# A pre-LN attention and GeGLU block: placement of group 0's keys and queries, FFN chunks, Tanh GELU and the last slot changed

## The chip, the cores and the metric

The kernel runs on one core of one Trainium2 chip. The metric is the device time of one execution in microseconds (us), the median of several runs; lower is better. The engines of a core are named as in the profile: PE (TensorE, matmuls; PEld is its weight load), DVE (VectorE), ACT (ScalarE), POOL (GpSimd) and SP (SyncE, which here issues transfers). Each takes its instructions in the order in which the program lists them; between engines they wait on semaphores.

## The reference

One transformer block on x of 2048 rows and 640 columns in bf16, 32 heads of 20:

```python
def _A_ref(x, wqkv, wo):                       # H = 32, Dh = 20
    qkv = (x @ wqkv).reshape(B, S, 3, H, Dh).transpose(2, 0, 3, 1, 4)
    q, k, v = qkv[0], qkv[1], qkv[2]
    p = softmax(einsum("bhqd,bhkd->bhqk", q, k) * Dh ** -0.5)
    o = einsum("bhqk,bhkd->bhqd", p, v)
    return o.transpose(0, 2, 1, 3).reshape(B, S, D) @ wo

def _B_ref(x, w_gate, w_up, w_down):           # Df = 1728
    return (gelu_tanh(x @ w_gate) * (x @ w_up)) @ w_down

h = x + _A_ref(layernorm(x), wqkv, wo)
out = h + _B_ref(layernorm(h), w_gate, w_up, w_down)
```

## The kernel before

The program doesn't run loops on the chip. Python code lists every operation with its engine, an estimated length, a priority, its reads and writes and the PSUM banks that it takes and frees (`Sched.op`, which all operations pass through, so most lines of the profile are L403 or a helper's). `Sched.schedule` then plays a list scheduler through once: at each moment each engine takes the ready operation of the smallest priority (P_QK = 0 first, P_BG = 3 last), and the resulting order is written out, with semaphore waits, by `Sched.emit`. The order on the chip is therefore fixed; only the times are the chip's. When PE has too little to do the scheduler adds dummy matmuls (`warm`, `pad`) by the limits WARM_MIN and PAD_MIN. It keeps background matmuls off PE when the next QK is due, QK_LEAD before its exp.

The head: x comes in four loads of 512 rows, LayerNorm statistics are taken on DVE (for rows 512 to 1023 on ACT), applied on DVE into xn_p, transposed on PE and evicted to xnT by ACT or DVE (L650, L653). Then the keys and queries of head group 0 are projected (`proj_k`, `proj_q`, matmuls at L702, evictions at L737 and L740). Keys and queries lie in kt_all and qt_all as 32 rows for each of four heads: row 0 holds a constant, rows 1 to 20 the head's values. For group 0 they are copied there by SP transfers, four for each 512 keys and four for the queries. The query's row 0 is an upper bound of its scores, got from the largest key of each row (L730) and one matmul (L811), added by DVE at L815.

Attention: a group is four heads, a slot is 512 query x head-group units: all 2048 keys for one group and 512 queries, or two groups and 256, or four and 128. There are 32 slots of 64 tiles; a tile is 128 keys by 512 (queries x groups), one PSUM bank. QK tiles (L1001) go in turn to banks 0 to 2 and to banks 3 and 4 (in the slots of SIX to 0 to 2 and 3 to 5), and ACT takes one exp over all banks of a set, of 1536 or 1024 columns, into pts or pts2. Some quads (four tiles, one for each head) are done by DVE instead, with a polynomial (L925 and what follows); D_QUADS says how many in each slot. In the slots of DA_SLOTS the polynomial's last addition is done by a POOL transfer that accumulates, elsewhere by DVE. PV products gather in bank 6 (32 rows for each head, 21 columns of v of which the last is one); an epilogue copies bank 6 to osb, transposes it (L1098), divides (L1104, L1107) and writes o_nat.

FFN: when the last group of a query chunk is done, `post` transposes o_nat, multiplies by wo, adds x (L1146), takes LayerNorm, and lists the gate products (L1179, copied to SBUF at L1214), GELU, the up products (L1228) and the down products (`down`, L1259, L1263) as background work in the two or three banks that QK leaves. Chunks are SIZES = 512, five of 256, two of 128. GELU of a chunk is done on ACT in place, up to 2048 columns at a time, after all its gate products; MERGE puts chunk 1 with chunk 2. Gelu and exp need different tables, so each such visit is a table load, the gelus, and a table load. The last chunk (`tail`) runs after the last exp, with its gelu straight from PSUM (L1201, L1204). FFN weights lie over the attention's weights and xnT (regw); they are loaded after slot 7's projections.

Of the kernel before, what the change touches and what calls it, by code (L numbers as in the profile page):

```python
# [18 lines left out]
WARM_WIN, WARM_MIN = 3.4, 0.5  # L19
PAD_WIN, PAD_MIN = 3.4, 0.42  # L20
QK_LEAD = .65
PE_AGE = 1.5
SD_ALONE = .21
P_SD = 1
# [23 lines left out]
class Sched:  # L48
# [48 lines left out]
    def schedule(self):  # L97
# [23 lines left out]
        while done < total:  # L121
            assert events, "no operation can start"
# [3 lines left out]
            for e in ENGINES:  # L126
# [122 lines left out]
                for o in ([o, join] if join is not None else [o]):  # L249
                    o.start = t0 if o is chosen else free[e]  # L250
                    if e == "act":
                        due = t + o.dur + (0.905 if o.dur > 1.2 else 1.332) - QK_LEAD if o.mode == "exp" else None
# [27 lines left out]
    def emit(self, es, block_of):  # L280
# [3 lines left out]
        prog = {e: [] for e in ENGINES}  # L284
        for o in self.order:
# [8 lines left out]
            for d in o.deps:  # L294
                q = ops[d]
                if q.eng == "pe" and o.eng == "pe":
                    continue
                k, c = q.pos
                if k not in need or need[k].pos[1] < c:
                    need[k] = q  # L300
# [50 lines left out]
SIZES = (512, 256, 256, 256, 256, 256, 128, 128)  # L351
BASE = (0, 0, 2, 0, 2, 0, 2, 3)
SIX = tuple(range(8, 12))
CHUNKS = tuple((sum(SIZES[:i]), n) for i, n in enumerate(SIZES))
NF = (DFF + 127) // 128
# [10 lines left out]
D_LAG = 8  # L366
MERGE = (1,)
DA_ISSUE, DA_LAT = 0.95, 6.4
DA_SLOTS = (1, 2, 3, 5) + tuple(range(9, 32))
PR, PR2 = 12, 6  # L370
D_QUADS = (1,) + (2,) * 11 + (3, 2) * 3 + (2, 2, 3) * 3 + (2,) * 5
D_FIRST, D_PART = 2, 0.55
D_LEAD = ((0,) * 8, (0, 10, 20) + (36,) * 21)
D_WIDE = 18
RSQRT_MAGIC = float(0x5F3759DF)

P_EV = 1.8
P_QK, P_PV, P_PRO, P_EPI, P_LN, P_BG = 0, 1, 1.5, 2, 2.5, 3
P_LND, P_LNP = 1.9, 2.5


def bass_sequential_preLN__mha_block__glu_gated_geglu__prompt_kernel(
# [12 lines left out]
    with ExitStack() as es:  # L395
# [13 lines left out]
        def c_act(n):  # L409
            return 0.052 + n * 0.000833  # L410
# [8 lines left out]
        off0 = sb("off0", [128, 1], FP32)  # L419
        stats = sb("stats", [128, 4, 2, 6], FP32)  # L420
# [3 lines left out]
        asum = sb("asum", [128, 2, 4], FP32)  # L424
# [49 lines left out]
        xn_p = carve(4 * D).rearrange("p (i d) -> p i d", i=4)  # L474
# [50 lines left out]
        def cst(fn, key, n=128):  # L525
            op(POOL, fn, 0.1 + n * 0.001, P_BG, writes=[key, "pool"])
# [5 lines left out]
        op("act", I("activation", f32(qt_all[:, 1, :, :]), zer[:, 0:2].bitcast(FP32).to_broadcast([128, 2048]), ACT.Copy), 1.8, P_QK,  # L532
           reads=["zer"], writes=["qf1"])
        op("act", I("activation", f32(qt_all[:, 2, :, :]), zer[:, 0:2].bitcast(FP32).to_broadcast([128, 2048]), ACT.Copy), 1.8, P_QK,
           reads=["zer"], writes=["qf2"])
        op("act", I("activation", v_all[:, :, :, DH], zer[:, 0:1].unsqueeze(2).to_broadcast([128, NT, H]), ACT.Copy, bias=1.0), 0.5, P_QK,
           reads=["zer"], writes=["vones"])
        op("dve", I("memset", f32(kt_all[:, 1:4, :]), ones2), 4.2, P_QK, writes=["kf0"])
        cst(I("memset", kt_all[:, 0, :].bitcast(FP32), ones2), "ktm0", 1024)
# [815 lines left out]
```

## Time and profile before

| | us |
|---|---|
| median of 3 runs | 910.08 |
| lowest, highest | 909.8, 910.76 |
| span of the profiled execution | 906.4 |
| ACT busy | 877.0 (97%) |
| PE busy | 832.6 (92%) |
| DVE busy | 740.7 (82%) |
| POOL busy | 123.5 (14%) |

The span runs from the first to the last instruction of the profiled execution; no time of its own with what lies around it is shown, so the runs' median stands beside it, 3.7 above. Busy time is the union of an engine's instructions; a row of the timeline gives start, length, engine, line, operation, what is written and read, and in brackets how long the engine sat idle before it and which instruction ended that. A group's row gives count, busy time and mean length of one in ns. The granted clock of TensorE was 1.0 throughout.

### The profile page before, as it was taken

The numbers are of one execution on the slowest core, as the hardware profiler recorded it, in microseconds if no ns is written. First come the engines' busy times: TensorE is split into PE (matmuls) and PEld (weight loads), VectorE is DVE, ScalarE is ACT, GpSimd is POOL, SyncE is SP. The second block draws the span as 40 slices with busy tenths as digits, with TensorE's granted clock in tenths as the row PEclk, the third lists the DMA queues.
The fourth block names the chain that finished last, engine by engine and source line by source line (L and its number), as shares of the span: only waits on it lengthen the run. The fifth ranks groups of instructions, "written<-read, shape, count | busy, mean of one in ns | idle before, by whom it ended". The sixth has DMA issues, their size and how long they took to land.

```text
span 906.4 us, 25256 instructions
## 1 busy us (share of the span) xinstructions
PE 832.6 (92%) x11167; PEld 376.8 (42%) x11167; DVE 740.7 (82%) x1405; ACT 877.0 (97%) x793; POOL 123.5 (14%) x238
## 2 busy tenths in 40 slices
PE   3999999999898988999999999999999998998998
PEld 2432322222233332334344445444444444656666
DVE  8858898989899997898898877787977996778643
ACT  7899999999999999999999999999999999999992
POOL 5001110000013111111222000030101000101000
PEclk9999999999999999999999999999999999999999
DMA  7213341442634322243263221441432332242110
GB/s 261 84 32 80 69 97 31 106 105 62 198 136 77 56 52 48 48 69 73 49 115 63 48 44 29 84 85 41 93 63 43 75 69 39 58 85 56 33 41 16
DMA packets 52357, 65.97 MB, mean 73 GB/s; under 512 B 20876, under 2 KB 38376, under 8 KB 52248
## 3 DMA queue, kind: packets, MB, share of 16 engines
q0 software_dynamic: 12816, 31.46, 19.4%
q1 hardware_dynamic: 39432, 32.89, 13.2%
q8 instruction: 88, 1.44, 0.7%
q14 instruction: 21, 0.17, 0.1%
HBM read 20.12 MB, written 8.09 MB: 31 GB/s over the span
## 4 chain that ended last, share of the span: by engine, by line
ACT 82%; PE 13%; DVE 4%; POOL 1%; issue 0%
ACT pts L403 52%; ACT rege L403 28%; PE ps L702 4%; PE ps L1001 3%; PE ps L1179 2%; PE ps L403 2%; ACT L403 1%; PE ps L1259 1%; DVE dwx L403 1%; DVE qt_all L925 0%; PE ps L644 0%; DVE rege L1228 0%; ACT qt_all L403 0%; POOL nw L403 0%; DVE rege L925 0%
## 5 line engine op out<-in xcount | busy, mean ns | idle before, releaser
L403 ACT ACTIVATE pts<-ps 128x1536 bf16<-128x1536 f32 (+1 forms) x474 | 565.3, 1373 | 3.9 <-PE ps L403 2.9
L1001 PE MATMUL ps<-qt_all,kt_all 32*128 32x256 bf16 (+2 forms) x4096 | 308.9, 272 | 39.1 <-ACT pts L403 18.1
L403 ACT ACTIVATE rege<-ps 128x1536 bf16<-128x1536 f32 (+1 forms) x233 | 292.7, 1379 | 0.5 <-PE ps L403 0.4
L1001 PEld LDWEIGHTS ps<-qt_all,kt_all 32*128 32x128 bf16 x4096 | 102.4, 92 | 252.8 <-ACT pts L403 128.6
L1179 PE MATMUL ps<-rege,regw 128*128 128x256 bf16 (+2 forms) x1120 | 159.2, 274 | 10.2 <-ACT rege L403 2.7
L403 PE MATMUL ps<-pts,v_all 128*21 128x256 bf16 (+2 forms) x2370 | 124.8, 274 | 0.0
L1179 PEld LDWEIGHTS ps<-rege,regw 128*128 128x128 bf16 x1120 | 86.1, 98 | 62.5 <-issue 27.6
L925 DVE TENSOR_SCALAR rege<-ps 128x512 int16<-128x512 f32 x120 | 81.9, 686 | 22.2 <-PE ps L1001 21.1
L925 DVE TENSOR_SCALAR qt_all<-ps 128x512 int16<-128x512 f32 x104 | 71.2, 686 | 27.1 <-PE ps L1001 26.4
L403 PE MATMUL ps<-rege,v_all 128*21 128x256 bf16 (+2 forms) x1366 | 91.1, 278 | 0.1
L702 PE MATMUL ps<-regw 128*128 128x512 bf16 (+1 forms) x360 | 87.5, 353 | 1.9 <-ACT regw L650 1.5
L1259 PE MATMUL ps<-regw,rege 128*128 128x320 bf16 x448 | 83.8, 302 | 2.5 <-DVE qt_all L925 0.7
L403 DVE TENSOR_TENSOR qt_all<-qt_all 128x1024 int16<-128x1024 f16 (+3 forms) x77 | 68.7, 893 | 1.1
L403 PEld LDWEIGHTS ps<-pts,v_all 128*21 128x21 bf16 x2370 | 54.8, 91 | 32.7 <-issue 27.8
L403 DVE TENSOR_SCALAR qt_all<-qt_all 128x1024 int16<-128x1024 int16 (+3 forms) x106 | 57.9, 549 | 1.6 <-DMA qt_all<-dwx 0.4
L403 DVE TENSOR_TENSOR rege<-rege 128x1024 f16<-128x1024 f16 (+1 forms) x74 | 50.4, 681 | 0.7
L1259 PEld LDWEIGHTS ps<-regw,rege 128*128 128x128 bf16 x448 | 36.4, 98 | 35.0 <-issue 16.6
L403 PE MATMUL ps<-kt_all,zer 128*32 128x512 bf16 x568 | 48.3, 385 | 0.0
L403 DVE TENSOR_SCALAR rege<-rege 128x1024 int16<-128x1024 int16 (+2 forms) x113 | 47.8, 437 | 0.4
L702 PEld LDWEIGHTS ps<-regw 128*128 128x128 bf16 x360 | 28.9, 99 | 44.1 <-issue 24.4
L1214 DVE CAST rege<-ps 128x512 bf16<-128x512 f32 (+1 forms) x53 | 35.9, 678 | 13.3 <-PE ps L1179 13.1
L1228 DVE TENSOR_TENSOR rege<-rege,ps 128x512 bf16<-128x512 bf16 (+1 forms) x53 | 35.7, 676 | 12.2 <-PE ps L1179 12.1
(114 smaller groups left out, 766.2 us busy)
## 6 DMA issues: line engine op xcount, KB each, us to landing
qt_all<-qt_all POOLq DMA_DIRECT2D x9, 512.0 KB, 5.0
qt_all<-dwx POOLq DMA_DIRECT2D x9, 512.0 KB, 4.6
rege<-rege POOLq DMA_DIRECT2D x16, 256.0 KB, 3.5
rege<-dwx POOLq DMA_DIRECT2D x7, 512.0 KB, 4.8
rege<-in_A_x_dram SPq DMA_DIRECT2D x5, 640.0 KB, 5.7
dvx<-qt_all POOLq DMA_DIRECT2D x6, 512.0 KB, 4.8
q_rows<-regw SPq DMA_DIRECT2D x20, 128.0 KB, 2.8
out_dram<-rege SPq DMA_DIRECT2D x16, 160.0 KB, 3.2
```

The source lines that it names most:

```text
L403: return lambda eng: getattr(eng, method)(*args, **kwargs)
L702: yield op("pe", lambda eng, l=l, r=r, k=k: eng.matmul(bank(bk, n), l, r, start=(k == 0), stop=(k == len(steps) - 1)), c_mm(n) + cold, pri ...
L925: d_ops.append(op("dve", lambda eng: eng.tensor_scalar(v[:, 512 * h:512 * h + 512], bank(b), EXP_MUL, -32000.0, ALU.mult, ALU.max), c_dve( ...
L1001: return lambda eng: eng.matmul(out()[:, kk * nq:(kk + 1) * nq], kt_all[32 * j:32 * j + 32, g, kt * 128:(kt + 1) * 128], qt_all[32 * j:32 ...
L1179: op("pe", lambda eng, a=a, f=f, fi=fi: eng.matmul(bank(bk)[:, fi * nq:(fi + 1) * nq], w[:, a, F0[f]:F0[f] + 128], hnT[:, a, 128 * tb:128 ...
L1214: cp.append(op("dve", lambda eng, bg=bg, fv=fv, w=w: eng.tensor_copy(fv, bank(bg, w)), c_dve(w), p, reads=[kg], writes=hkeys(k), rel=[bg], ...
L1228: hdone.append(op("dve", lambda eng, bu=bu, fv=fv, w=w: eng.tensor_tensor(fv, fv, bank(bu, w), ALU.mult), c_dve(w), p, reads=[ku] + hkeys( ...
L1259: op("pe", lambda eng, f=f, o=o, hf=hf, bk=bk: eng.matmul(bank(bk, 320), ha_f[:, o:o + 128], wd[:, f, hf * 320:(hf + 1) * 320], start=(f = ...
```

## The change

- *Group 0.* The queries and the last 512 keys (PERM_C = 3: keys from 1536 on) are put into the 32-row layout by a matmul with a permutation matrix `perm`; for the queries it accumulates in the bank of the bound. Keys 0 to 1535 are still copied by transfers. wk, wq and wv are loaded apart, wk first, and K's last 512 keys of group 0 are projected tile by tile.
- *Head.* LayerNorm statistics: of each four tiles the last 1, 1, 3 and 1 on ACT (LN1_ACT). Seven tiles are applied on POOL (LN1_POOL), nine evictions of xnT are on DVE (T_DVE), xn_p has eight buffers, small LayerNorm operations go to POOL. The fills of qt_all that ACT did go to POOL behind the applies, with the fills of kt_all's groups 4 to 7.
- *Chunks and slots.* SIZES = seven of 256 and two of 128. Slots 0 to 5 are groups 0 to 5 with 512 queries, slots 6 and 7 groups 6 and 7 with queries 0 to 255 and 256 to 511, so chunk 0 can be posted after slot 6. SIX is empty. The last slot is split: groups 4 to 6, then group 7 alone. D_QUADS sums to 70 (before 69); DA_SLOTS has 19 slots (before 27).
- *Weights.* w_gate is laid over wv, wk and k_un and asked for in slot 4 in pieces; w_up and w_down follow in pieces after slot 7.
- *GELU.* MERGE = (0, 2). For chunks 4, 6 and 7 (TANH) it is 0.5 g (1 + tanh(...)) with the polynomial on DVE and one Tanh for each bank of 512 columns on ACT, in rounds of the buffers that qt_all lends.
- *Order.* The last chunk's work has priority P_END = 0.5; its eviction of transposes is on DVE, wo's first four contraction steps run before the last group is there, and the down matmuls don't wait for the last product. The root of the LayerNorm takes eps as a bias. Constants of the scheduler change (WARM_MIN, PAD_MIN, QK_LEAD, PE_AGE, D_LAG and priorities), and POOL operations now wait for the one before.

```diff
-WARM_WIN, WARM_MIN = 3.4, 0.5
-PAD_WIN, PAD_MIN = 3.4, 0.42
-QK_LEAD = .65
-PE_AGE = 1.5
+WARM_WIN, WARM_MIN = 3.4, 0.53
+PAD_WIN, PAD_MIN = 3.4, 0.46
+QK_LEAD = 0.55
+PE_AGE = 0.5
...
-                        due = t + o.dur + (0.905 if o.dur > 1.2 else 1.332) - QK_LEAD if o.mode == "exp" else None
+                        due = t + o.dur + (0.905 if o.dur > 1.2 else 1.332) - QK_LEAD if o.mode == "exp" and o.tag[0] == "P" else None
...
-SIZES = (512, 256, 256, 256, 256, 256, 128, 128)
-SIX = tuple(range(8, 12))
+SIZES = (256,) * 7 + (128, 128)
+SIX = ()
+PERM_C = 3
+FIRST = 6
+QR = ((0, 512),) + CHUNKS
-D_LAG = 8
-MERGE = (1,)
+D_LAG = 4
+MERGE = (0, 2)
+TANH = (4, 6, 7)
+W_EARLY = 4
+P_END = 0.5
+P_LATE = 3
+P_TANH = -1
-DA_SLOTS = (1, 2, 3, 5) + tuple(range(9, 32))
-D_QUADS = (1,) + (2,) * 11 + (3, 2) * 3 + (2, 2, 3) * 3 + (2,) * 5
+DA_SLOTS = (0, 1, 10, 11, 12, 14, 15, 16, 17, 18, 19, 20, 22, 23, 24, 26, 27, 28, 31)
+D_QUADS = (0, 2, 2, 2, 2, 2, 2, 1, 2, 2, 2, 2, 3, 2, 3, 2, 3, 2, 3, 2, 3, 2, 3, 2, 3, 1, 4, 2, 3, 2, 2, 2, 0)
+T_DVE = (0, 1, 3, 5, 9, 11, 12, 13, 14)
+LN1_ACT = (1, 1, 3, 1)
+LN1_POOL = (0, 1, 3, 5, 6, 13, 14)
-P_EV = 1.8
+P_EV = 1.5
-P_LND, P_LNP = 1.9, 2.5
+P_LND, P_LNP = 1.7, 1.9
...
-        op("act", I("activation", f32(qt_all[:, 1, :, :]), zer[:, 0:2].bitcast(FP32).to_broadcast([128, 2048]), ACT.Copy), 1.8, P_QK,
-           reads=["zer"], writes=["qf1"])
...
+        for g in range(4, NG):
+            cst(I("memset", kt_all[:, g, :].bitcast(FP32), ones2), "kf%d" % g, 800, e_ops)
+        for k in range(1, 4):
+            for g in range(0, NG, 2):
+                cst(I("memset", f32(qt_all[:, k, g:g + 2, :]), 0.0), "qf%d%d" % (k, g), 512, e_ops)
...
+                e_ops.append(ln_apply(POOL if t in LN1_POOL else "dve", x_sb[:, t, :], xn_p[:, t % 8, :], ("xnp", t % 8), t, [f"x{t // 4}"], P_PRO,
                                       first=True))
...
+            if t == 0 and c == 3:
+                for tt in range(4):
+                    for a in range(NA):
+                        w_readers.append(op("pe", lambda eng, tt=tt, a=a: eng.matmul(
+                            bank(bk)[:, 128 * tt:128 * tt + 128], wsrc[:, a, 0:128], xnT[:, a, c * 512 + 128 * tt:c * 512 + 128 * tt + 128],
...
+                if t == 0 and c >= PERM_C:
+                    w_readers.append(op("pe", lambda eng, bp=bp, src=src: eng.matmul(bank(bp), perm[:], src, start=True, stop=True), c_mm(512), prio,
+                                        mode="full", util=0.213, reads=[("ku", 0, c), "perm"], writes=[kp], acq=[bp]))
+                    dst = kt_all[:, 0, 512 * c:512 * c + 512]
...
+            w_readers.append(op("pe", lambda eng: eng.matmul(bank(bk), perm[:], q_un[:, 0, :], start=True, stop=False),
...
-            q_first.append(op("dve", lambda eng: eng.scalar_tensor_tensor(
-                out=dst, in0=bank(bk), scalar=off0[:, 0:1], in1=dst, op0=ALU.add, op1=ALU.add), c_dve(512) + 0.05, prio,
+            q_first.append(op("dve", lambda eng: eng.tensor_scalar(dst, bank(bk), off0[:, 0:1], None, ALU.add), c_dve(512), prio,
...
-        for c, (q0, nq) in enumerate(CHUNKS):
+        for c, (q0, nq) in enumerate(QR):
             n = 512 // nq
-            slots += [(c, tuple(range(g, g + n))) for g in range(0, NG, n)]
+            slots += [(c, tuple(range(g, g + n))) for g in (range(FIRST) if c == 0 else range(FIRST if q0 < 512 else 0, NG, n))]
+        slots[-1:] = [(slots[-1][0], slots[-1][1][:-1]), (slots[-1][0], slots[-1][1][-1:])]
...
+            elif c in TANH:
+                for k0 in range(0, nb, nt_):
+                    for k in range(k0, min(k0 + nt_, nb)):
+                        bg, kg = mms(k, wg, "wg", tuple(x for key in hkeys(k) for x in sc.rd.get(key, ())))
+                        op("dve", lambda eng, bg=bg, fv=fv, w=w: eng.tensor_scalar(fv, bank(bg, w), 0.5, None, ALU.mult), c_dve(w), p, reads=[kg],
+                           writes=hkeys(k), rel=[bg], after=first)
+                        d(I("tensor_tensor", z, f2, f2, ALU.mult), 0.53, hkeys(k), [tk], aft)
+                        d(I("tensor_scalar", z, z, 8 * 0.044715 * GELU_C, 2 * GELU_C, ALU.mult, ALU.add), 0.265, [tk], [tk])
+                        d(I("tensor_tensor", z, z, f2, ALU.mult), 0.53, hkeys(k) + [tk], [tk])
+                        tanhs.append(op("act", I("activation", z, z, ACT.Tanh), c_act(w) + 0.04, P_TANH, mode="exp", reads=[tk], writes=[tk]))
+                    for k in range(k0, min(k0 + nt_, nb)):
+                        bu, ku = mms(k, wu, "wu", (sc.lw[tk],))
+                        op("dve", lambda eng, bu=bu, z=z, w=w: eng.scalar_tensor_tensor(
+                            out=z, in0=z.bitcast(F16), scalar=1.0, in1=wide(bank(bu, w)), op0=ALU.add, op1=ALU.mult), c_dve(w), p,
+                           reads=[ku, tk], writes=[tk], rel=[bu])
+                        hdone.append(op("dve", I("tensor_tensor", wide(fv), wide(fv), z, ALU.mult), 0.066 + 0.53 * w / 1024, p,
+                                        reads=[tk] + hkeys(k), writes=hkeys(k)))
...
+                if g == W_EARLY:
+                    pieces(wg, B_w_gate.rearrange("(a p) f -> p a f", p=128), "wg", tuple(w_readers))
```

344 lines of the change are left out of this document (209 added, 135 removed).

## The prediction

> **What bounds the kernel now.** I read the page first, then the busy time by stage, then ACT's instructions by shape, then the chain of waits at both ends.
>
> ```profile
> span 906.4 us, 25256 instructions
> ...
> PE 832.6 (92%) x11167; PEld 376.8 (42%) x11167; DVE 740.7 (82%) x1405; ACT 877.0 (97%) x793; POOL 123.5 (14%) x238
> ...
> L403 ACT ACTIVATE pts<-ps 128x1536 bf16<-128x1536 f32 (+1 forms) x474 | 565.3, 1373 | 3.9 <-PE ps L403 2.9
> ...
> L403 ACT ACTIVATE rege<-ps 128x1536 bf16<-128x1536 f32 (+1 forms) x233 | 292.7, 1379 | 0.5 <-PE ps L403 0.4
> ```
>
> ACT is busy for 97% of the span, and its 474 + 233 = 707 exps are nearly all of it. The stages, cut at the first exp and at the end of the last:
>
> ```profile
> core 0: us, PE busy (x) PEld busy (x) DVE busy (x) ACT busy (x) POOL busy (x), PEclk, DMA share, GB/s
> 0.00:32.86 32.86, 18.43 (x138) 10.71 (x138) 27.93 (x82) 27.49 (x48) 12.83 (x36) 1.00 0.58 195
> 32.86:876.01 843.15, 788.99 (x10700) 345.91 (x10699) 701.25 (x1295) 838.60 (x731) 110.63 (x202) 1.00 0.33 70
> 876.01:906.40 30.39, 25.15 (x331) 20.15 (x330) 11.55 (x30) 10.91 (x14) 0.00 (x0) 1.00 0.04 13
> ```
>
> In the middle ACT idles 843.15 - 838.60 = 4.55 us. So three things set the time: the head (32.86), ACT's own list in the middle, and the tail (30.39).
>
> **The middle, term by term.** From the chain of waits (start, length, what) and ACT's timeline and shapes:
>
> ```profile
> 742.85 4.52 ACT pts L403 x4
> ...
> 874.65 1.34 ACT rege L403
> ```
> ```profile
> L403 ACT ACT_TABLE_LOAD x16 | 20.5, 1283 | 1.1 <-PEq L1340 0.8
> L403 ACT ACTIVATE rege<-rege 128x2048 bf16<-128x2048 bf16 x8 | 15.0, 1904 | 0.1
> ...
> L403 ACT ACTIVATE rege<-rege 128x1536 bf16<-128x1536 bf16 x5 | 7.3, 1467 | 0.0
> ...
> L1201 ACT ACTIVATE dvx<-ps 128x512 bf16<-128x512 f32 x3 | 1.8, 597 | 4.7 <-PE ps L1179 4.7
> ```
> ```profile
> 539.54 1.28 ACT L403 ACT_TABLE_LOAD   x1
> 540.83 6.46 ACT L403 ACTIVATE rege<-rege 128x2048 bf16<-128x2048 bf16 x4
> 547.31 1.28 ACT L403 ACT_TABLE_LOAD   x1
> ```
>
> Two exps of three banks and two of two banks take 4.52, so a pair takes 2.26; a three-bank exp alone advances the chain by 1.34, a two-bank one by 0.92: each further bank costs 0.427, an instruction by itself 0.063. Laying out the tiles by SIZES, PAT and D_QUADS gives 358 exps of three banks and 349 of two before (707, as on the page), worth 800.1 us. With the new lists it gives 354 and 353: the list sums to 70 DVE quads against 69 (although the title says 69), so four tiles of 0.427 leave ACT: **-1.7**. SIX goes, but its three-bank pairs were worth only the 0.063 of the instructions they spared, which these counts hold.
>
> Gelu: four instructions over 2 x 2048 + 2 x 1536 = 7168 columns took 6.46, so 256 query rows (3584 columns) cost 3.23. Before the last exp the old kernel gelus 1792 rows = 7 such, 22.6; the new one 1280 rows = 5 such: **-6.5**. The 512 rows of chunks 4 and 6 become 14 Tanh of one bank; by the pitch above 0.063 + 0.427 = 0.49 each, and chunk 7 gives 3.5 more (it was a gelu after the last exp): **+8.6**. The nearest single row, L1201's 512 columns, is 0.597 with its own drain, so the upper end is +10.5.
>
> Table loads: 16 in all, one ahead of the head, one for the first exp, four after the last exp, so ten in the middle: five gelu visits of two. MERGE (0,2) and TANH (4,6,7) leave three visits (chunks 0+1, 2+3, 5): four loads of 1.28 fewer, **-5.1**, and the drain beside each, (838.6 - 800.1 - 22.6 - 12.8) / 10 = 0.31: **-1.2**. The lower end is the loads alone. The row prices a switch at 1.28 + 0.31. The Trainium skill (ScalarE: Activation LUTs, "What ACT_TABLE_LOAD costs") gives about 2.66 for every switch, drain included; by that the four would be worth 10.6, not 6.3; the measured lines decide.
>
> Sum of ACT's list: 838.6 - 1.7 - 6.5 + 8.6 - 5.1 - 1.2 = 832.7. Idle time:
>
> ```profile
> 42.23 4.63 ACT L403 ACTIVATE pts<-ps 128x1536 bf16<-128x1536 f32 x4 [2.48 <-PE ps L403]
> ```
>
> This one stall is over half of the 4.55. The seventh exp reuses the first slots of pts and waits for the first PV, which stands behind V projections that hold bank 6 until DVE empties it. Slot 0 now has no DVE quad, so DVE empties it sooner; I take the stall away and put 2 us for Tanhs that stand at ACT's head before DVE's polynomial is done: 4 in all, bounds 2 and 10. **Middle: 836.7.**
>
> What hides the rest is DVE's slack. Each Tanh bank adds four SBUF operations on 512 columns, and 24 quads instead of 9 lie outside DA_SLOTS and add on DVE again:
>
> ```profile
> 560.00:876.00 316.00, 300.28 (x5119) 162.53 (x5111) 247.59 (x401) 315.48 (x276) 38.17 (x82) 1.00 0.31 62
> ```
> ```profile
> L403 DVE TENSOR_TENSOR rege<-rege 128x1024 int16<-128x1024 int16 x14 | 9.5, 681 | 0.1
> ```
>
> At half of 0.68 the Tanh banks cost 18 x 4 x 0.34 = 24.5, and nine of the fifteen quads fall here, two adds each: 12.3. That is 284 of 316, below ACT's 315; at the full 0.68 it would be 309, and the cover is gone.
>
> **The head.** DVE, ACT and PE lines, in time order:
>
> ```profile
> 2.19 3.69 ACT L403 ACTIVATE qt_all<-zer 128x2048 f32<-128x2048 f32 x2
> ...
> 22.40 5.47 ACT L650 ACTIVATE regw<-ps 128x640 bf16<-128x640 bf16 x9
> ```
> ```profile
> 22.19 1.57 DVE L403 TENSOR_SCALAR rege<-rege,mu,rs 128x640 bf16<-128x640 bf16 x4 [0.94 <-PE ps L644]
> ...
> 27.35 0.49 DVE L653 COPY regw<-ps 128x640 bf16<-128x640 bf16 x1
> ...
> 29.82 0.68 DVE L730 TENSOR_REDUCE kd<-ps 128x1 f32<-128x512 f32 x1
> ...
> 31.53 0.75 DVE L815 SCALAR_TENSOR_TENSOR qt_all<-ps,off,qt_all 128x512 bf16<-128x512 f32 x1 [0.30 <-PE ps L811]
> ```
> ```profile
> 27.15 3.98 PE L702 MATMUL ps<-regw 128*128 128x512 bf16 x22
> ```
> ```profile
> L403 ACT ACTIVATE rege<-rege 128x640 bf16<-128x640 bf16 x8 | 6.2, 770 | 0.1
> ```
>
> ACT and DVE both work nearly without a gap until the last xnT is evicted at 27.84; then come K's matmuls, the peak, the bound, the first QK: 5.0 more. ACT loses the two fills (3.69) and six evictions of 5.47/9 = 0.61 (3.65) and gains two tiles of statistics, four passes of 0.77 and their read-outs (3.5): net -3.8. DVE loses seven applies of 1.57/4 = 0.39, two tiles of statistics and most small operations, and gains six evictions of 0.49: net about -2. The 0.94 wait for a free xn_p buffer goes with eight of them. I put the last eviction 2.3 earlier, the engine with the smaller relief deciding. Behind it K's matmuls for keys 512 to 1535 no longer stand, and the last 512 keys go tile by tile: of the 22 matmuls (0.18 each) some ten leave, 1.7. **First exp at 28.9, -4.0.** POOL's seven applies are not in this trace; the nearest rows are the 0.39 on DVE and POOL's 0.95 for a fill of 1024, so 0.6 by length, and I take no delay. Lower end nothing gained, if POOL is late with them; upper end -6.4, ACT's whole 3.8 plus 0.94 and 1.7. The permutation matmul itself replaces four q copies and four K copies on SP and turns the 0.75 into a plain add; with the keys it places needed only at tile 48 and later, it shortens the path by next to nothing. The fills moved behind the applies on POOL are needed only when group 1 starts, 29 us after the first exp (slot 0's exps); they take 4 x 0.95 + 12 x 0.55 = 10.4:
>
> ```profile
> L403 POOL MEMSET kt_all<- 128x1024 f32 x5 | 4.8, 951 | 0.3
> ...
> L403 POOL MEMSET qt_all<- 128x512 f32 x7 | 3.8, 550 | 0.4
> ```
>
> **The tail.** Chain of waits after the last exp:
>
> ```profile
> 878.82 1.71 ACT rege L403
> ...
> 881.36 1.43 PE ps L702 x10
> ...
> 885.71 0.93 DVE rege L1228 x2
> ...
> 886.72 3.28 PE ps L1259 x23
> ...
> 891.07 8.01 PE ps L1179 x140
> ...
> 899.58 3.99 PE ps L1259 x28
> ```
>
> The gelu, L1228 and the x23 are the second-last chunk's FFN, in the way of the last chunk's residual, LayerNorm and eviction: 1.71 + 0.93 + 3.28 = 5.9 of the chain. I give back 1.5 for steps of the last chunk that ran beneath them (transposes, root, apply): 4.4. With its FFN at P_LATE against P_END = 0.5, with no table visit, and with the chain of FFN chunks starting earlier, that goes. The chunks run one behind another, and the first gate matmuls stand here:
>
> ```profile
> 280.00:305.00 25.00, 6.65 (x22) 1.49 (x22) 1.00 0.38 68
> ```
>
> The 25 us before hold none. With weights requested at slot 4 they can begin at slot 8, whose begin the exps of slots 0 to 7 put at 28.9 + 208 = 237, so some 45 us are won against a lag that the last chunk still feels. Splitting the last slot leaves one group for the end: of the ten wo matmuls two remain (-1.1), and copy, transposes, scale and eviction shrink by about 1.8. The down matmuls no longer wait for the last product (-0.1 to -0.5). **Tail: 30.4 - 4.4 - 2.9 - 0.1 = 23.0**, bounds 22 and 27 (only the split).
>
> **Sum.** 28.9 + 836.7 + 23.0 = 888.6 against the span of 906.4, 17.8 less. The three runs have a median of 910.08, 3.7 above the span, which I keep: **892.3**. Changes under 0.2% (1.8 us) can't be told from none.
>
> **The rivals.**
>
> *Half of it* (20%): POOL's applies are late, so the head stays at 32.9, and FFN backlog still spills behind the last exp, 27: 32.9 + 836.7 + 27 + 3.7 = 900.3. For it: DVE falls out of DA_SLOTS more often, so background products slow down. By the Trainium skill (SBUF — State Buffer, "Who interferes with whom") a DVE operation in a two-port mode blocks GpSimd for its whole length, which speaks against applies on POOL beside DVE's; no row here shows it.
>
> *QK comes too late* (6%), slower. QK_LEAD falls from 0.65 to 0.55, so background matmuls may run 0.1 us further into the gap before a QK:
>
> ```profile
> 746.51 0.40 PE L1001 MATMUL ps<-qt_all,kt_all 32*128 32x256 bf16 x6
> ```
> ```profile
> 746.98 2.65 ACT L403 ACTIVATE rege<-ps 128x1536 bf16<-128x1536 f32 x2
> ```
> ```profile
> PEld ps L1001 <- ACT pts L403: 128.6, 351, 1.6
> ```
>
> Here the QK ended 0.07 before its exp began, so 0.1 later would hold ACT. At 0.06 for each of the 354 three-bank exps that is 21 us: 888.6 + 21 + 3.7 = 913. It turns the sign from 17.8/354 = 0.05 each. Against it: 351 times PE already stood waiting for ACT, 0.37 on average, so most gaps aren't filled up to the limit.
>
> *Tanh isn't in exp's table* (2%): then the change doesn't save loads but adds up to 18 pairs of 1.6, 58 us: some 950. The trace has no Tanh. The Trainium skill (ScalarE: Activation LUTs, "Table sets: the hidden batching unit") lists tanh in exp's set, which is why this stays small.
>
> **How the numbers follow.** Forecast 70% (own range 886 to 898 from the bounds of head, idle and tail), half of it 20%, slower ways 8%, some other way to no change 2%. Range 885 to 904. Faster 0.9, within 0.2% 0.02, slower 0.08.
>
> **What would show it.** First exp near 29; 10 table loads instead of 16 and none between a Tanh and an exp; 354 + 353 exps at 2.26 a pair; ACT idle between first and last exp under 6; last exp to end near 23, with no gate or up matmul of the second-last chunk in it. It is wrong if ACT's idle sum passes 10 (QK or Tanh late), or if the first exp isn't earlier.

## The result, and the profile after

The changed kernel takes 898.77 us (897.65 to 899.58) against 909.98 before on the same chip, a ratio of 0.9876 (95% interval 0.9862 to 0.989). It is faster, by 11.2 us where 17.8 were predicted, and 6.5 us above the predicted 892.3. From the page, the span and the engines:

```profile
span 897.2 us, 26288 instructions
...
PE 837.0 (93%) x11645; PEld 401.2 (45%) x11679; DVE 773.3 (86%) x1452; ACT 864.7 (96%) x799; POOL 123.4 (14%) x244
```

The busy time by stage, cut as before at the first exp and at the end of the last (columns: stretch, length, busy PE, PEld, DVE, ACT, POOL, granted clock, DMA share, GB/s):

```profile
0.00:32.38 32.38, 19.58 (x152) 12.35 (x156) 25.72 (x64) 24.95 (x50) 23.09 (x60) 1.00 0.58 190
32.38:869.50 837.12, 792.63 (x11172) 368.29 (x11201) 735.19 (x1358) 834.30 (x741) 100.33 (x185) 1.00 0.30 62
869.50:897.20 27.70, 24.83 (x325) 20.51 (x323) 12.35 (x31) 5.45 (x10) 0.00 (x0) 1.00 0.08 26
```

| stage | before | predicted | after |
|---|---|---|---|
| head, to the first exp | 32.86 | 28.9 | 32.38 |
| middle, first exp to end of the last | 843.15 | 836.7 | 837.12 |
| of it ACT's list / ACT idle | 838.60 / 4.55 | 832.7 / 4 | 834.30 / 2.82 |
| tail | 30.39 | 23.0 | 27.70 |

The middle came out as the sum said. Head and tail gave 3.2 us together where 11.4 were expected: that is where the missing gain lies. By these spans the gain is 9.2 us, not 11.2. The profile of before is one of its fastest executions: in the executions whose span is on record before takes 1.7 to 2.2 us more than its span, so its median belongs to a span of about 908, against 906.4 here. ACT's instructions by shape show the middle's terms one by one:

```profile
L426 ACT ACTIVATE pts<-ps 128x1536 bf16<-128x1536 f32 x236 | 364.9, 1546 | 2.1 <-PE ps L426 1.3 <-PE ps L1065 0.4
L426 ACT ACTIVATE pts<-ps 128x1024 bf16<-128x1024 f32 x236 | 265.1, 1123 | 0.0
L426 ACT ACTIVATE rege<-ps 128x1536 bf16<-128x1536 f32 x118 | 181.7, 1540 | 0.3 <-PE ps L1065 0.3
L426 ACT ACTIVATE rege<-ps 128x1024 bf16<-128x1024 f32 x117 | 131.1, 1121 | 0.0
L426 ACT ACT_TABLE_LOAD x10 | 12.8, 1283 | 1.0 <-PEq L1465 0.8
L426 ACT ACTIVATE qt_all<-qt_all 128x512 f16<-128x512 f16 x17 | 11.4, 690 | 0.2 <-DVE qt_all L426 0.2
```

236 + 118 = 354 exps of three banks and 236 + 117 = 353 of two, and ten table loads, as predicted. The last row is the Tanh. The idle column of the exps has 0.4 + 0.3 us behind QK (L1065), so the shorter QK_LEAD doesn't hold ACT. On ACT's timeline no table load stands between a Tanh and its exps, for example:

```profile
855.28 1.47 ACT L426 ACTIVATE pts<-ps 128x1536 bf16<-128x1536 f32 x1
856.61 0.65 ACT L426 ACTIVATE qt_all<-qt_all 128x512 f16<-128x512 f16 x1
857.13 3.30 ACT L426 ACTIVATE pts<-ps 128x1024 bf16<-128x1024 f32 x3
```

**The head after**, on ACT, DVE and PE (start, length, instruction, idle time before it):

```profile
24.96 0.70 ACT L680 ACTIVATE regw<-ps 128x640 bf16<-128x640 bf16 x1 [0.55 <-PE ps L674]
...
29.72 0.69 ACT L801 ACTIVATE kt_all<-ps,one 128x512 bf16<-128x512 f32 x1 [0.48 <-PE ps L796]
30.31 0.76 ACT L881 ACTIVATE v_all<-ps 128x320 bf16<-128x320 f32 x2
31.09 1.28 ACT L426 ACT_TABLE_LOAD   x1
32.38 2.36 ACT L426 ACTIVATE pts<-ps 128x1536 bf16<-128x1536 f32 x2
```
```profile
25.26 1.27 DVE L773 TENSOR_REDUCE kd<-regw 128x1 f32<-128x512 bf16 x2
...
27.60 0.67 DVE L773 TENSOR_REDUCE kd<-ps 128x1 f32<-128x512 f32 x1
...
29.51 0.75 DVE L868 TENSOR_SCALAR qt_all<-ps,off 128x512 bf16<-128x512 f32 x1
```
```profile
30.65 0.60 PE L1065 MATMUL ps<-qt_all,kt_all 32*128 32x512 bf16 x5
```

The same load and the first QK before the change, on ACT and on PE:

```profile
31.48 1.28 ACT L403 ACT_TABLE_LOAD   x1
```
```profile
32.43 0.59 PE L1001 MATMUL ps<-qt_all,kt_all 32*128 32x512 bf16 x5
```

The last xnT eviction ends at 25.66, 2.2 us earlier than before (27.87), and the first QK begins 1.8 earlier. But the exp doesn't follow it: ACT, in its own order, still has the eviction of the placed keys, two V evictions and the table load. Before, the load ended (32.76) while the first QK ran; now it ends (32.37) 1.1 us after the five matmuls of the first QK have. So the exp begins 1.73 us behind the begin of the first QK, where it was 0.43 before.

**The tail after**, on PE, from 875.57 on, with the last chunk's residual already taken (L1267 gate and up, L1382 down, L674 the transposes of the last chunk's normalized rows):

```profile
875.57 1.56 PE L1267 MATMUL ps<-rege,regw 128*128 128x128 bf16 x25
876.96 0.44 PE L674 MATMUL ps<-ident,o_nat 128*128 128x128 bf16 x5
877.24 2.79 PE L1267 MATMUL ps<-rege,regw 128*128 128x128 bf16 x47
879.89 2.08 PE L1382 MATMUL ps<-regw,rege 128*128 128x320 bf16 x14
881.81 0.94 PE L1267 MATMUL ps<-rege,regw 128*128 128x128 bf16 x14
882.63 2.07 PE L1382 MATMUL ps<-regw,rege 128*128 128x320 bf16 x14
884.54 5.99 PE L1267 MATMUL ps<-rege,regw 128*128 128x128 bf16 x104
890.36 3.97 PE L1382 MATMUL ps<-regw,rege 128*128 128x320 bf16 x28
```

The last chunk's own FFN is 140 gate and up and 28 down matmuls. The 25 at 875.57, 25 of the 165 from 877.24 on and the two groups of 14 downs are the second-last chunk's, in a tail in which PE is busy 24.83 of 27.70.

### The profile page after: what moved, and what is told of

Same layout as the page of the kernel before. It is cut to its first block, busy times and chain, and to the rows that moved or that the text cites. A ratio compares the mean times of both kernels' runs of the same rounds, so it can differ in the third digit from the quotient of the medians.

```text
span 897.2 us, 26288 instructions
## 1 busy us (share of the span) xinstructions
PE 837.0 (93%) x11645; PEld 401.2 (45%) x11679; DVE 773.3 (86%) x1452; ACT 864.7 (96%) x799; POOL 123.4 (14%) x244
## 4 chain that ended last, share of the span: by engine, by line
ACT 66%; PE 20%; DVE 9%; DMA 2%; POOL 1%; issue 1%
ACT pts L426 42%; ACT rege L426 22%; PE ps L1065 5%; PE ps L737 4%; PE ps L1382 3%; PE ps L426 3%; PE ps L1267 3%; DVE qt_all L426 3%; DVE qt_all L989 1%; DMA rege<-o_nat 1%; ACT L426 1%; DVE stats L426 1%; DVE dwx L426 1%; POOL nw L426 1%; PE ps L674 1%
## 5 line engine op out<-in xcount | busy, mean ns | idle before, releaser
L426 ACT ACTIVATE pts<-ps 128x1536 bf16<-128x1536 f32 x472 | 558.9, 1335 | 2.1 <-PE ps L426 1.3
L1065 PE MATMUL ps<-qt_all,kt_all 32*128 32x256 bf16 (+2 forms) x4224 | 315.4, 269 | 28.6 <-ACT pts L426 14.3
L426 ACT ACTIVATE rege<-ps 128x1536 bf16<-128x1536 f32 x235 | 289.6, 1331 | 0.3 <-PE ps L1065 0.3
L1065 PEld LDWEIGHTS ps<-qt_all,kt_all 32*128 32x128 bf16 x4224 | 107.0, 92 | 229.0 <-ACT pts L426 106.7
L1267 PE MATMUL ps<-rege,regw 128*128 128x256 bf16 (+1 forms) x1260 | 160.4, 262 | 5.8 <-ACT rege L426 2.4
L1267 PEld LDWEIGHTS ps<-rege,regw 128*128 128x128 bf16 x1260 | 98.9, 98 | 54.6 <-issue 28.7
L1382 PE MATMUL ps<-regw,rege 128*128 128x320 bf16 x448 | 80.5, 301 | 1.1 <-DVE qt_all L989 0.5
L989 DVE TENSOR_SCALAR rege<-ps 128x512 int16<-128x512 f32 x108 | 73.2, 685 | 9.4 <-PE ps L1065 8.8
L426 DVE TENSOR_TENSOR qt_all<-qt_all 128x1024 f16<-128x1024 f16 (+5 forms) x86 | 78.5, 913 | 1.1
L426 DVE TENSOR_SCALAR qt_all<-qt_all 128x2048 int16<-128x2048 int16 (+4 forms) x130 | 66.5, 517 | 1.5 <-DMA qt_all<-dwx 0.2
L426 PE MATMUL ps<-kt_all,zer 128*32 128x512 bf16 x648 | 56.4, 385 | 0.7 <-DVE osb L426 0.6
L1382 PEld LDWEIGHTS ps<-regw,rege 128*128 128x128 bf16 x448 | 37.2, 97 | 29.9 <-issue 14.9
L426 PEld LDWEIGHTS ps<-rege,v_all 128*21 128x21 bf16 x1392 | 37.8, 91 | 22.1 <-issue 15.1
L737 PEld LDWEIGHTS ps<-regw 128*128 128x128 bf16 x350 | 27.7, 98 | 40.7 <-issue 22.4
L989 DVE TENSOR_SCALAR dvx<-ps 128x512 int16<-128x512 f32 x60 | 40.6, 683 | 3.9 <-PE ps L1065 3.7
## 6 DMA issues: line engine op xcount, KB each, us to landing
regw<-in_A_wqkv_dram SPq DMA_DIRECT2D x3, 800.0 KB, 11.2
```

The lines of the kernel that those rows point to most:

```text
L426: return lambda eng: getattr(eng, method)(*args, **kwargs)
L737: yield op("pe", lambda eng, l=l, r=r, k=k: eng.matmul(bank(bk, n), l, r, start=(k == 0), stop=(k == len(steps) - 1)), c_mm(n) + cold, pri ...
L989: d_ops.append(op("dve", lambda eng: eng.tensor_scalar(v[:, 512 * h:512 * h + 512], bank(b), EXP_MUL, -32000.0, ALU.mult, ALU.max), c_dve( ...
L1065: return lambda eng: eng.matmul(out()[:, kk * nq:(kk + 1) * nq], kt_all[32 * j:32 * j + 32, g, kt * 128:(kt + 1) * 128], qt_all[32 * j:32 ...
L1267: op("pe", lambda eng, a=a, f=f, fi=fi: eng.matmul(bank(bk)[:, fi * nq:(fi + 1) * nq], w[:, a, F0[f]:F0[f] + 128], hnT[:, a, 128 * tb:128 ...
L1382: op("pe", lambda eng, f=f, o=o, hf=hf, bk=bk: eng.matmul(bank(bk, 320), ha_f[:, o:o + 128], wd[:, f, hf * 320:(hf + 1) * 320], start=(f = ...
```

## Experiments

The theory behind the first ones: the head ends on ACT's queue, and the tail on the second-last chunk's FFN (chunk 7). Stages by profile, with the way from the last xnT eviction on ACT to the first exp in a column of its own. In eight kernels with the head unchanged (after, e1, e2, e3, e6, e7, e8, e11) that way is 7.41 or 7.42, while the eviction itself moves between 24.06 and 25.01, so the head's steps are compared by this column and not by the first exp. In these eight the first exp lies between 31.48 and 32.42; the 32.38 of the table above is among the late ones, and the whole head gained 0.4 to 1.4 us against the one profile of before.

| kernel | median us | xnT to exp | middle | ACT's list | tail |
|---|---|---|---|---|---|
| after | 898.77 | 7.42 | 837.12 | 834.30 | 27.70 |
| e1_no_ffn7 | 890.16 (one execution) | 7.42 | 834.26 | 832.00 | 22.66 |
| e2_unmerge | 898.94 | 7.42 | 838.52 | 835.01 | 27.66 |
| e3_all_gelu | 904.46 | 7.41 | 839.52 | 836.97 | 30.77 |
| e4_v_on_dve | 897.33 | 6.51 | 840.42 | 834.49 | 27.65 |
| e5_load_early | 896.83 | 6.12 | 836.82 | 834.33 | 27.60 |
| e6_no_split | 904.17 | 7.41 | 835.17 | 832.05 | 34.61 |
| e7_tanh_last_only | 903.50 | 7.41 | 840.02 | 837.48 | 29.81 |
| e8_fewer_pads | 899.80 | 7.41 | 835.71 | 832.84 | 30.02 |
| e9_load_and_v | 897.76 | 6.51 | 836.48 | 834.16 | 27.64 |
| e10_applies_on_dve | 897.93 | 5.89 | 839.35 | 834.68 | 27.63 |
| e11_lead_back | 899.07 | 7.41 | 834.63 | 833.04 | 30.47 |
| e12_keys_by_transfer | 897.89 | 7.11 | 836.39 | 834.17 | 27.55 |

Four executions of the changed kernel lie between 897.65 and 899.58, so I don't tell medians apart below some 2 us and go by the stages. Each stage is from one profiled execution.

**e1: chunk 7's FFN left out.**

```diff
+            if c == len(CHUNKS) - 2:
+                tt, t = tb, q0 // 128
...
+                return
             p = P_LATE if c == len(CHUNKS) - 2 else P_BG
```

> Leaves out the FFN of chunk 7 (rows 1792 to 1919: gate, Tanh, up and down products; its output rows are h). After the last exp the changed kernel's PE still does the down products of chunk 6, the up products of chunk 7 (70 of 0.056 us) and its down products (28 of 0.137 us). Theory backlog (the 27.7 us after the last exp are long because FFN products left over stand on PE in front of or between the last chunk's): 70 x 0.056 + 28 x 0.137 = 7.7 us go, the tail falls to 20 to 22, the span from 897.2 to about 889. Rival own chain (the last chunk's steps from PV to the output set the tail, the left-over products only fill gaps): the tail stays above 26 and only ACT's 1.8 us of Tanh go, span about 895.

The tail falls by 5.0 to 22.66 (7.7 were expected, and a tail of 20 to 22). On PE, the transposes, then the last chunk's gate and up in one run, then its downs:

```profile
872.41 0.45 PE L674 MATMUL ps<-ident,o_nat 128*128 128x128 bf16 x5 [1.11 <-DVE o_nat L426]
...
873.45 7.99 PE L1275 MATMUL ps<-rege,regw 128*128 128x128 bf16 x140
881.27 3.97 PE L1390 MATMUL ps<-regw,rege 128*128 128x320 bf16 x28
```

The 140 begin 873.45 - 865.74 = 7.7 us behind the last exp; the prediction's 23.0 holds the same 7.7 (23.0 less the 15.3 that follow in before). So the predicted tail is that of a kernel whose chunk 7 has been worked off, and its FFN is what was left over. The run takes the chunk's work off PE, DVE and ACT alike, so by itself it doesn't say which engine held it up.

**e2: the chunks' gelus merged as before, so that no chunk waits for its partner.**

```diff
-MERGE = (0, 2)
-TANH = (4, 6, 7)
+MERGE = (0,)
+TANH = (2, 4, 6, 7)
```

> Chunk 2 takes the Tanh path and isn't merged with chunk 3 any more (MERGE = (0,), TANH = (2, 4, 6, 7)), so its up products need not wait for chunk 3's gates. Theory lag by merging (the FFN falls behind because chunk 2 stands from its gates at 405 to 430 us until chunk 3's gelu at 515, and the lag is still there at the end): chunks 4 to 7 start 20 to 40 us earlier, the tail falls from 27.7 to 22 to 24, ACT's list grows by 0.5, the time falls by 3 to 5 us. Rival (the lag is a matter of what PE and DVE can do beside attention, and seven more Tanh banks add some 9 us to DVE): chunk 6 and 7 start as late as before, the tail stays at 27 or more, the time is the same or up to 2 us longer.

Nothing moves in the tail: 27.66, as the rival had it. Waiting for a partner chunk isn't the cause of the backlog.

**e3 and e7: Tanh away altogether, and from chunks 4 and 6 only.**

```diff
-TANH = (4, 6, 7)
+TANH = ()        # e3
+TANH = (7,)      # e7
```

> TANH = (): chunks 4, 6 and 7 go back to gelu in place, each with a table visit of its own, all else as changed. Theory ACT's list (Tanh is worth what it saves on ACT): chunks 4 and 6 cost 2 x 3.23 instead of 14 x 0.52, chunk 7 1.7 instead of 1.9, and six table loads of 1.28 + 0.31 come back: first to last exp and the rest grow by 8 to 9.5 us, the time by as much. Rival DVE relief (four SBUF operations for each bank leave DVE, 18 banks, about 25 us, so the FFN lags less): part of it comes back in the tail, which falls under 25, and the time grows by less than 6.

> Chunks 4 and 6 use the Gelu table, chunk 7 alone keeps Tanh. ACT's list between first and last exp grows by two gelus of 3.23 and four loads of 1.6 and loses 14 Tanhs of 0.52: +5.6 us. DVE loses some 20 us between 600 and 869 us. Theory (the backlog that spills behind the last exp piles up because DVE is full from 760 to 820 us): tail at most 25, time 899 to 902. Rival (PE's own work holds the FFN up): tail 27 to 28.5, time 903.5 to 905.

Both are slower, 904.46 (0.9941 of before, 0.9918 to 0.9963) and 903.50 (0.9929, 0.991 to 0.9948). The middle and the tail of e3, then of e7:

```profile
31.51:871.03 839.52, 801.30 (x11186) 367.31 (x11184) 716.72 (x1288) 836.97 (x731) 100.16 (x185) 1.00 0.30 62
871.03:901.80 30.77, 26.08 (x361) 21.58 (x358) 12.29 (x29) 9.71 (x12) 0.00 (x0) 0.99 0.05 18
```
```profile
31.77:871.79 840.02, 801.82 (x11197) 367.76 (x11195) 718.12 (x1292) 837.48 (x732) 100.20 (x185) 1.00 0.30 62
871.79:901.60 29.81, 25.99 (x351) 21.03 (x348) 15.34 (x42) 10.86 (x16) 0.00 (x0) 1.00 0.05 18
```

DVE has 735.19 - 716.72 = 18.5 and 17.1 us less in the middle than after the change, and the tail doesn't fall; it rises by 3.1 and 2.1. So the tail of at most 25 that less DVE work should bring didn't come, and DVE's load isn't shown to hold chunk 7 up. The first row of gates of chunk 7 stands at 847.83 in e3 and 848.02 in e7, after the change at 847.79. ACT has 9.71 and 10.86 us in these tails against 5.45: the gelu of chunk 7 in e3, its last Tanhs in e7, which slip behind the last exp and bring table loads with them. So Tanh is worth 5.7 us in all (904.46 - 898.77), some 2.4 in the middle and 3.1 in the tail; the 8 to 9.5 expected of e3 was too much.

**e6: the last slot not split.**

```diff
-        slots[-1:] = [(slots[-1][0], slots[-1][1][:-1]), (slots[-1][0], slots[-1][1][-1:])]
```

(One entry less in D_QUADS and D_LEAD.)

> The last slot holds two groups again, as before the change. Theory of the prediction (the split takes 2.9 us from the chain behind the last exp): tail 30 to 31 us, time about 901.5. Rival (behind the last exp PE works off the FFN of the second-last chunk in any case, and the split only shortens what is hidden beneath): tail 27.5 to 28.5, time within 1 us of 898.8.

904.17 us (0.9935, 0.9919 to 0.9951). Tail 34.61, more than the theory's 30 to 31; the rival falls. The two kernels' roots of the last LayerNorm on ACT's timeline, e6 first:

```profile
876.89 0.30 ACT L426 ACTIVATE sd<-mv,eps 128x1 bf16<-128x1 bf16 x1 [5.94 <-DVE mv L426]
```
```profile
875.47 0.30 ACT L426 ACTIVATE sd<-mv,eps 128x1 bf16<-128x1 bf16 x1 [4.45 <-DVE mv L426]
```

That is 9.3 us behind the last exp (867.59) against 6.0 (869.50): 3.3 us, near the 2.9 that the prediction gave for the split. The other 3.6 of the 6.9 I put down to the backlog: without the single group at the end, Tanhs of chunk 7 stand behind the last exp (ACT 10.31 us in the tail), and the middle is 2.0 shorter for it.

**e8: fewer fillers; e11: QK_LEAD as before.**

```diff
-PAD_WIN, PAD_MIN = 3.4, 0.46
+PAD_WIN, PAD_MIN = 3.4, 0.42     # e8
-QK_LEAD = 0.55
+QK_LEAD = 0.65                   # e11
```

> PAD_MIN goes back from 0.46 to 0.42, so fewer filling matmuls (kt_all, zer) are added: about 560 instead of 648, some 8 us less on PE in all. Theory (PE holds the FFN up): chunk 7's matmuls come earlier and the tail falls to 26 to 27, time 897 to 898. Rival (DVE or the two background banks hold it up): tail within 0.4 of 27.7 and the time as it was. If the fillers were needed, the granted clock falls below 0.99 in some stage and the time rises.

> QK_LEAD goes back from 0.55 to 0.65. Theory (the shorter lead costs nothing, since ACT waited for a QK only 0.4 us in all): ACT's idle time between first and last exp stays under 4, time 898 to 900. Rival (the shorter lead lets the FFN into gaps that it would else miss): the tail grows by over 1 us and the time goes over 900. Third (the lead holds ACT): the middle falls below 836.

e8 takes away far fewer of these fillers than expected, 20 of 648, and another group of them (kt_all alone) grows from 54 to 73, so it says nothing of PE's share. Both make the middle shorter (835.71, 834.63) and the tail longer (30.02, 30.47), with the sum, 865.7 and 865.1, within 1 us of 864.8: again Tanhs of chunk 7 change sides of the last exp. e11's time is 899.07: the shorter lead costs nothing and, by the sum, gains nothing that can be measured.

**e4, e5, e9: the queue of ACT ahead of the first exp.** e4 evicts the first four V products on DVE; e5 gives ACT a one-column exp behind its eviction of the third 512 keys (25.44, by the timeline its fourth K or Q eviction, not the fifth), so that the table load stands there; e9 does both.

```diff
-proj_v(kt, 0, (6, 7, 5), P_EPI if kt < 4 else P_BG, "act" if kt < 4 else "dve")
+proj_v(kt, 0, (6, 7, 5), P_EPI if kt < 4 else P_BG, "dve")                        # e4, e9
+op("act", I("activation", nm[:, 1:2], eps[:], ACT.Exp), 0.06, P_PRO, reads=["eps"],
+   writes=["warmexp"], after=(sc.lw[("ku", 0, 2)],))                              # e5, e9
```

> The first four V evictions go from ACT to DVE. In the changed kernel the first QK has its operands at about 30.3 us, but ACT still evicts K's permuted keys and V until 31.07 and then loads exp's table for 1.28, so the first exp starts at 32.38. Theory ACT's queue (the first exp is late because of what stands on ACT in front of its table load): without 1.6 us of V evictions the load starts earlier and the first exp comes at 30.9 to 31.6. Rival QK (the first QK itself sets it): the first exp stays at 32.2 or later.

> ACT is given one exp of a single column behind its fifth K or Q eviction, so the table load that stood between the V evictions and the first exp (31.09, 1.28 us) falls into ACT's idle time near 27 us. Theory (ACT's own queue ends the head): the first exp comes 0.8 to 1.3 us earlier, at 31.1 to 31.6, and the middle and the tail stay as they are: a time of about 897.6. Rival (the key peaks on DVE and the matmuls behind them end the head): the load only delays other evictions, and the first exp stays at 32.2 or later.

> The two edits that moved the first exp, together: the table load early and the V evictions of the head on DVE. Theory (ACT's queue ended the head, then the first QK does): the first exp follows the first QK at once, at 29.5 to 30.2, and with middle and tail as after the change the time is 895.5 to 896.8. Rival (DVE pays for the V evictions in front of the key peaks or in slot 0): first exp at 30.4 or later, or the time no better than 896.8.

ACT in e5, and its first QK on PE:

```profile
24.36 0.70 ACT L680 ACTIVATE regw<-ps 128x640 bf16<-128x640 bf16 x1 [0.54 <-PE ps L674]
...
26.05 1.28 ACT L426 ACT_TABLE_LOAD   x1
...
30.48 4.62 ACT L426 ACTIVATE pts<-ps 128x1536 bf16<-128x1536 f32 x4
```
```profile
30.04 0.60 PE L1065 MATMUL ps<-qt_all,kt_all 32*128 32x512 bf16 x5
```

From the eviction to the first exp 6.12 instead of 7.42: 1.30 gained, the load's own length, and none given back (middle 836.82, tail 27.60). ACT's queue did end the head. The exp now begins 0.44 behind the begin of the first QK (30.04), as it did before the change (0.43), so e5 has taken out all that ACT's queue cost there. e4 gains 0.90, but its first QK comes later behind the eviction (6.08 instead of 5.69), and its exp stands 0.43 behind that QK. In e9 the gains don't add, as the rival had it; ACT and DVE there:

```profile
31.48 4.62 ACT L426 ACTIVATE pts<-ps 128x1536 bf16<-128x1536 f32 x4 [1.39 <-PE ps L1065]
```
```profile
28.21 0.48 DVE L884 CAST v_all<-ps 128x320 bf16<-128x320 f32 x1
...
30.10 0.75 DVE L868 TENSOR_SCALAR qt_all<-ps,off 128x512 bf16<-128x512 f32 x1
```

ACT now waits 1.39 for QK, since DVE puts V evictions between the key peaks and the bound. The next bound behind ACT's queue is the first QK, with DVE's chain ahead of it. e5, 896.83 us (0.9851, 0.9836 to 0.9866), is the best of all; its 1.9 us under the changed kernel's median is about what can be told apart, and 1.30 of it is in the trace.

**e10: all applies of the first LayerNorm on DVE.**

```diff
-LN1_POOL = (0, 1, 3, 5, 6, 13, 14)
+LN1_POOL = ()
```

> LN1_POOL is empty: all sixteen applies of the first LayerNorm on DVE at 0.39 to 0.5 each, none on POOL at 0.9 to 1.0. Theory (DVE is the busier of the two, POOL's slowness lies beside it): DVE gets some 3 us more in front of the last xnT and the first exp comes 1 to 3 us later, at 33 to 35. Rival (the last two applies on POOL, 22.30 to 24.30, are what the last xnT waits for): the first exp comes 0.3 to 1 us earlier, at 31 to 31.7.

```profile
27.53 0.70 ACT L680 ACTIVATE regw<-ps 128x640 bf16<-128x640 bf16 x1 [1.04 <-PE ps L674]
...
33.42 3.71 ACT L426 ACTIVATE pts<-ps 128x1536 bf16<-128x1536 f32 x3
```

The last eviction comes at 27.53, 2.5 later than the latest seen with POOL's help, and the first exp at 33.42. POOL's slow applies don't end the head: with all of them on DVE this profile's first exp is 1.0 to 1.9 later than in the eight above. The medians (897.93 and 898.77) don't show the loss, so that the applies on POOL save time isn't shown.

**e12: group 0's last 512 keys by transfers again.**

```diff
-PERM_C = 3
+PERM_C = 4
```

> PERM_C goes from 3 to 4: group 0's last 512 keys are placed by transfers again, as the other keys; the queries keep the permutation matmul. Theory of the prediction (these keys are needed 20 us after the first exp, so placing them by matmul buys nothing) joined with ACT's queue as the head's end: ACT loses the eviction of 0.69 (29.72) ahead of the table load, the first exp comes 0.5 to 0.7 us earlier measured from the last xnT eviction (7.42 us behind it after the change, 6.7 to 6.9 here), and no exp of group 0 waits for a transfer. Rival (the transfers of these keys are late): ACT waits for PE's QK somewhere between 45 and 60 us by over 1 us more, and the time rises by as much.

7.11 from eviction to exp: 0.3 gained where 0.5 to 0.7 was expected, since V evictions that had followed the keys' eviction without a gap now wait for PE. No exp of group 0 waits for a transfer, the only stall up to 60 us being the 1.19 for PV that was there. No gain from placing these keys by a matmul is shown; the way to the first exp is 0.3 longer with it.

## Why the prediction was right and wrong

The time, 898.77, lies inside the stated range of 885 to 904, but nearer to the rival "half of it" (900.3) than to the forecast (892.3).

**Middle: right, term by term but one.** 836.7 forecast, 837.12 measured; DVE between 560 us and the last exp 279 of 309.5 us where 284 of 316 was worked out. ACT's list is 1.6 longer than forecast; a Tanh advances ACT by 0.52 (856.61 to 857.13) and not 0.49, 18 times, which is 0.5 of it. The stall of 2.48 is a stall of 1.19, not gone, and Tanhs waited 0.2 us at ACT's head, not 2, so idle time is 2.82. The load is 1.28 in every row, but the 0.31 of drain beside it was too much. In a gelu visit after the change the exp ahead ends at 309.36 and the next begins at 318.44; less the gelus' 6.46 that is 2.6 for two loads, 1.3 each, and about 1.4 with the 0.1 by which an exp would otherwise overlap the next. e5 moved one load and the first exp by 1.30. The four drains come to 0.3 or 0.4, not 1.2, which is most of the rest of the 1.6. (The 0.31 was a residue: at the prediction's own 2.26 a pair and 1.34 the old exps are 800.8, not 800.1.) The Trainium skill (ScalarE: Activation LUTs, "What ACT_TABLE_LOAD costs") gives about 2.66 for a switch; by that e5 would have gained twice as much. The same page of the Trainium skill ("Table sets: the hidden batching unit") has exp and tanh in one set; the trace agrees, ten loads in all with 18 Tanhs among the exps.

**Head: -0.5 in place of -4.0.** The step "the last eviction 2.3 earlier" held (2.2; up to 3.1 in the other profiles with this head). The step that failed is the next, "Behind it ... 1.7": the stretch from that eviction to the first exp didn't fall from 5.0 to 3.3 but rose to 6.7. The prediction counted matmuls and the work of DVE there and left ACT's own queue out: evictions and the load that before lay beside the matmuls. Of the 3.4 missing, 1.30 is the wait of the first exp behind the first QK (1.73 instead of 0.43), and e5 shows it. The other 2.1 lies ahead of that QK, which begins 4.99 behind the eviction where it was 4.56 before and 2.9 was forecast. The matmuls that leave bought nothing there: those of the last keys end at 27.12, but DVE works off four key peaks one behind another (25.26 to 28.28), so the last peak ends 2.6 behind the eviction, as before. That DVE's order is the reason is argued from these rows; e9 shows that this chain comes next, and no run shortened it. The seven applies on POOL took 0.88 to 1.03 each, not the guessed 0.6; e10's later first exp speaks for them all the same.

**Tail: -2.7 in place of -7.4.** The failed step is "4.4 ... that goes", with its reason that 45 us won at the first chunk are still felt by the last. e1 prices the FFN of chunk 7 behind the last exp at 5.0, and 27.7 - 5.0 is the forecast 23.0 within 0.3. Its first gates, on PE's weight load and on PE, and the sum of the stretches from 840 to the last exp:

```profile
847.13 0.23 PEld L1267 LDWEIGHTS ps<-rege,regw 128*128 128x128 bf16 x4 [0.37 <-DMA rege<-o_nat]
```
```profile
847.79 1.07 PE L1267 MATMUL ps<-rege,regw 128*128 128x128 bf16 x16
```
```profile
sum 29.50, PE 28.35 PEld 20.32 DVE 22.65 ACT 28.78 POOL 1.83; mean PE 4.73 PEld 3.39 DVE 3.78 ACT 4.80 POOL 0.31
```

And the same chunk's first gates before the change:

```profile
868.46 0.95 PE L1179 MATMUL ps<-rege,regw 128*128 128x128 bf16 x14
```

The lead was won and it did reach the end: the first chunk's first gate moved from 289.75 to 243.17, and the second-last chunk's from 7.6 us before the end of the last exp to 22.4. What it can't do is bring chunk 7's FFN ahead of chunk 7's own inputs. The weight load at 847.13 waits for the chunk's transposed rows. Their transfer, issued at 841.0, landed 6.1 later, behind residual and LayerNorm (six us of small operations on POOL, 833.99 to 840.06), and the chunk's last attention output was written at 820.7. In the 22 us that are left chunk 6's ups and downs still stand, and PE is busy 28.35 of the 29.50 us from 840 on. So two things are argued from these rows and tested by no run: that chunk 7's chain from 820.7 to 847.1 comes too late, and that PE is too full behind it. From 820.7 to the last exp PE's idle time (2.0) and fillers (2.2) come to 4.2 us; by that estimate an earlier start could move about so much work ahead of the last exp. Merging (e2) is ruled out, and less DVE work (e3, e7) didn't shorten the tail. The split of the last slot was sized rightly where it was reasoned (3.3 against 2.9) and was worth about as much again (6.9 in the tail, 5.0 net of the middle) for what it keeps ahead of the last exp. By medians Tanh is worth 5.7 (e3) and the split 5.4 (e6), 11.1 of the 11.2 if the two add, which no run tested; neither did a run take the new chunk sizes or the early weights away.

**The rivals.** "Half of it" (900.3) has head and tail nearly as they came, 32.9 and 27, and its backlog of FFN behind the last exp is what e1 shows. Its reasons were others: POOL's applies were not late in the sense that mattered (e10), and less DVE work didn't shorten the tail (e3, e7). "QK comes too late" fell with the 0.7 us of ACT's waits for QK and with e11. "Tanh isn't in exp's table" fell with the ten loads. Last, 3.7 us were kept outside the span; the profiled execution took 899.02, 1.8 above its span. So the forecast span, 888.6, was missed by 8.6 us, and 1.9 of that is hidden in the time by luck.

## What to carry to other kernels

When an engine that runs in order gets its first important instruction earlier, list what else stands ahead of it in its own queue: a table load that was free beside a wait can become the wait, and a one-column instruction of the next table, placed in an idle stretch, takes it out. A lag that is won at the start of a chain of chunks is only worth at the end what the last links can use. Ask when the second-last chunk's inputs are ready and how full the engine is from there on. Work that can fall on either side of the last critical instruction moves time between two stages; judge such variants by the sum of the stages.

## What the runs showed of the hardware

In e4's profile the granted clock fell, to 0.50 and then 0.67, right behind a stretch in which PE was idle nearly half the time (columns as above, four microseconds each; from 712 on it is 1.00 again):

```profile
700.00:704.00 4.00, 2.14 (x35) 0.91 (x27) 3.40 (x4) 3.07 (x4) 0.31 (x1) 0.97 0.06 12
704.00:708.00 4.00, 4.00 (x35) 1.37 (x34) 1.38 (x2) 2.61 (x3) 0.59 (x1) 0.50 0.69 131
708.00:712.00 4.00, 4.00 (x44) 1.73 (x44) 1.88 (x4) 2.65 (x3) 0.00 (x0) 0.67 0.01 4
```
```profile
702.78 0.70 PE L1267 MATMUL ps<-rege,regw 128*128 128x256 bf16 x5 [1.67 <-DMA rege<-o_nat]
```

PE, in order, stood 1.67 us at a gate matmul that waited for a transposing transfer; then the clock was 0.50, and ACT lost 4.00 - 2.61 + 4.00 - 2.65 = 2.7 us in these eight, which is most of what e4's middle is longer. The changed kernel has the same wait at the same place, 0.59 us long, and no dip. e10's profile has one of 1.5 us there and a dip to 0.50, and two of its six executions took 902.1 us against 897.4 to 898.0 for the others. e8 waits 1.4 us for such a transfer at another place (846.7) and has no dip. That the wait brings the fall isn't shown: e2's profile has a clock of 0.61 from 456 to 460 with no wait of PE above 0.71 us in the twelve before, and the changed kernel has PE busy for only 2.12 of 4.00 us from 515 to 519 and keeps its clock. The profiled executions of e4 and e10 are 3 to 5 us longer than those of the same kernels with a clock of 1.00; what decides is open. The Trainium skill (TensorE: Matmul & The Clock Gate, "HAM oscillation — how this bites in real kernels") puts the rule as no idle gaps of TensorE over some 3.4 us. Here the longest gap ahead of a fall was 1.67, so the measurement asks for more care than the rule.

DVE's applies took 0.53 each where two stood beside two of POOL's (22.65 to 23.71, POOL 22.30 to 24.30), and 0.38 in a row of four in e10, where POOL has none. That fits what the Trainium skill (SBUF — State Buffer, "Who interferes with whom") says of the two engines' shared port; no run measured it by itself.
